# Reordering the last chunks of a convolution stage, moving one tap of two chunks to ScalarE and GpSimd, and issuing two sums earlier

## The chip, the cores and the metric

The kernel runs on one core of a Trainium2 chip. The metric is the device time of one execution in microseconds (us), and the number that counts is the median over the runs. In what follows PE is TensorE (the matrix engine), DVE is VectorE, ACT is ScalarE, POOL is GpSimd, and SP is the engine that only issues DMAs. Each works through its own list of instructions in order and waits for the others by semaphores.

## The reference, cut to what matters

The input `x` is (8, 6400, 128): eight batches, 6400 time steps, 128 channels. First a causal convolution of the full length with a filter `h` (done with FFTs in the reference), then a short convolution of five taps that makes a gate, and a gated projection:

```python
y = np.fft.irfft(np.fft.rfft(x, n=L, axis=1) * np.fft.rfft(h, n=L, axis=0)[None], n=L, axis=1)[:, :S, :]
gate_pre = sum(conv_w[k] * xp[:, k:k + S, :] for k in range(5))   # xp: y with 4 zeros in front
out = ((1 / (1 + np.exp(-gate_pre))) * (y @ w_val)) @ w_out
```

All data is float32.

## The kernel before

**The stages.** A sequence of 6400 is laid out as 100 x 64. For each batch the transform runs in four matmul stages. Stage 1 (`Forward`, lines 240 to 284) takes sums and differences of the two halves of an `x` tile (`sums`, on POOL) and multiplies them (`half`). Stage 2 (`Product`) multiplies by constants, DVE multiplies the result by the spectrum of `h`, and POOL adds the cross terms. Stage 3 (`s3_quads`) goes back. Stage 4 (`Chunk.s4`) gives the convolved sequence in 13 chunks: `HEAD` with 4 of the 64 rows (numbers 60 to 63) and twelve chunks of 5 rows, named by their first row 0, 5, ..., 55. A row is 100 time positions, so a chunk is 128 x 500.

**Two alternating loops per batch.** Lines 643 to 663 run 16 steps. Step g does stage 3 of this batch, stage 1 of the next batch (`fx.half`, `fx.sums`), and pieces of the gate work that the previous batch left over (`steps[g]`). Lines 693 to 736 then run 15 slots s. Slot s does stage 2 of the next batch in 13 blocks (blocks 11 and 12 in slots 7 and 8) and stage 4 of this batch, one chunk a slot, in an order that line 670 makes. In the seven batches that have a successor that order is 60, 0, 35, 40, 45, 50, 55, 5, 10, 15, 20, 25, 30, so that slots 7 to 12 have the chunks 5, 10, 15, 20, 25, 30. The end of this loop, from slot 7 on, is called the tail here; it comes before step 0 of the next loop of 16 steps.

**What a chunk does.** The result of `s4` stands in PSUM. In the same slot `copies` lets ACT copy it to SBUF (`act(self.y, self.p)`) and, unless the chunk is `late` (25 and up), scale it by tap 4 into the gate rows a+4 to a+8 (`init`) and by tap 3 into a spare tile `q` (`keep`). One slot later `taps` lets DVE add taps 0, 1 and 2, read from PSUM, to the gate rows a to a+6. Two slots later `add` lets POOL add `q` to the rows a+3 to a+7. So neighbouring chunks write overlapping gate rows and have to follow each other. A late chunk does only the copy in its slot; its `init`, `keep`, `taps` and `add` run in the steps of the next loop (chunk 25 in steps 0 and 1, 30 in steps 2 and 3, and so on), from the SBUF copy. `HEAD` and chunks 10, 15, 20 (`held`) and the late ones get their projection (`project`), sigmoid (`sigm`), product (`gate`), output matmul (`output`) and store in the steps too (tables `VALUE` and `OUTPUT`). Chunk 5 gets them in slots 10 and 11: in slot 10 PE projects it, ACT takes its sigmoid before the copies of that slot, DVE makes its gate product at the slot's end; in slot 11 PE makes its output.

**What orders the work.** Every instruction keeps the program's order on its engine. PSUM has four buffers of 128 x 500 for `s4`, `project`, `output` and the two results of `half` (`single`), and two double ones for stages 2 and 3 (`pair`). A buffer is taken again when its last reader is done: for a chunk that is not late this is its last DVE tap, for a late one its ACT copy, for a projection its gate product. The SBUF tile `h_sb[3]` holds spectrum block 11 until POOL has used it in slot 7, and its two halves hold the copies that `keep` inside `s3_quads` makes in even and odd steps; `h_sb[0]` holds the `q` tiles of chunks 15 (first half) and 20 (second half), and in steps 0 and 1 ACT issues the DMAs that reload these halves (`ahead`, line 305). `fx.sums` also issues the load of a further `x` tile on SP's queue. The first two sums of the loop of 16 steps (for its steps 0 and 1) are issued at the ends of slots 9 and 10 (line 735), the others inside the steps, always two steps ahead.

Of the kernel before, what the change touches and what calls it, by code (L numbers as in the profile page):

```python
# [17 lines left out]
N1 = 100  # L18
# [12 lines left out]
CH = 5  # L31
HEAD = (60, 4)
CHUNKS = [HEAD] + [(a, CH) for a in range(0, 60, CH)]
NCH = len(CHUNKS)
OUT_ORDER = CHUNKS[1:] + [HEAD]
LATE = 35
HELD = 10
WAIT = 25
BL = 2 * SB * C
M2B = 3  # L40
MH = 6
HB = 4
XB = 3
XH = 8
VALUE = {10: 0, 15: 1, 20: 2, 25: 4, 30: 5, 35: 6, 40: 8, 45: 10, 50: 12, 55: 14}
OUTPUT = {10: 2, 15: 3, 20: 4, 25: 6, 30: 7, 35: 8, 40: 9, 45: 11, 50: 13}
AHEAD = {
    0: (1, 0, 0), 1: (1, 0, 1), 4: (0, 0, 0), 5: (0, 0, 1), 7: (1, 1, 0), 8: (0, 1, 0),
    9: (0, 1, 1), 10: (0, 2, 0), 11: (0, 2, 1), 12: (1, 1, 1), 13: (1, 2, 0), 14: (1, 2, 1),
# [80 lines left out]
def longconv_moe(ctx: ExitStack, tc: tile.TileContext, x, h, r1, m2, r3, m4, w64, out):  # L130
# [26 lines left out]
    h_sb = [ring_at[M2B + i] for i in (2, 0, 1, 3)]  # L157
# [7 lines left out]
    p_t = [cp.tile([128, CH, N1], F32, name=f"p_{i}") for i in range(2)]  # L165
    keeps = p_t + [h_sb[0][:, i : i + CH * N1].rearrange("p (n t) -> p n t", t=N1) for i in (0, BL // 2)]
    rows = [t.rearrange("p a d n -> p (a d n)")[:, : CH * N1].rearrange("p (n t) -> p n t", t=N1) for t in sd_sb]
    hd = dp.tile([NKB, 128, 2 * SB * C], F32, name="hd")

    def weights():  # L170
# [69 lines left out]
    class Forward:  # L240


        def __init__(self, src, dst, xs=x_sb, o=0):
            self.src, self.dst, self.n, self.s, self.i, self.o = src, dst, 0, 0, 0, o
            self.xs = xs[o % len(xs) :] + xs[: o % len(xs)]
# [125 lines left out]
    def s3_quads(d0):  # L371
        pt = pair()
        for q in range(4):
            for c in range(2):
                for r, k in ((0, 0), (1, 0), (1, 1), (0, 1)):
                    d, o = k * HP + d0 + q, (r + k) % 2
                    w = d // 2 * 2 * N1 + c * 2 * HR + d % 2
                    v = pt[o * HP : (o + 1) * HP, k, q * 2 * N2 : (q + 1) * 2 * N2].rearrange("p (b m) -> p b m", b=2)
                    nc.tensor.matmul(
                        v[:, :, c::2],  # L380
                        lhsT=gyf[r * HP : (r + 1) * HP, w : w + 2 * HP - 1 : 2],
                        rhs=r3_sb[r * HP : (r + 1) * HP, c, :],
                        start=True,
                        stop=True,
                    )
        v = pt.rearrange("p k (d b m) -> p b m k d", b=2, m=N2)
        a = d0 // 4 % 2 * 512
        t = h_sb[HB - 1][:, a : a + 512]
        o = dv.rearrange("p n c (k d) -> p (n c) k d", k=2)[:, :, :, d0 : d0 + 4]

        def keep():
            act(
                t.rearrange("p (m c d) -> p m c d", c=2, d=2 * XG)[:, :, ::-1],
                pt.rearrange("p k (d b m c) -> p b m c (k d)", b=2, m=N2 // 2, c=2)[:, 1],
            )

        def join(op, n):
            u = t.rearrange("p (m k d) -> p m k d", k=2, d=XG)
            nc.vector.tensor_tensor(out=n, in0=v[:, 0, 2:], in1=u[:, 2:], op=op)

        def ends():
            act(o[:, 0:2], v[:, 0, :2])
            act(o[:, N2 : N2 + 2], v[:, 1, :2])

        return keep, ends, lambda: join(ADD, o[:, 2:N2]), lambda: join(ALU.subtract, o[:, : N2 + 1 : -1])
# [26 lines left out]
    class Chunk:  # L432


        def __init__(self, b, i, ch, defer):
            self.b, self.i, self.ch = b, i, ch
            a, n = ch
            self.defer = defer
            self.late = defer and WAIT <= a < HEAD[0]
            self.held = defer and HELD <= a < WAIT  # L440
            self.r = None
            self.y = yl[a][:, :n] if a >= LATE else held_y[a] if a >= HELD else dv[:, a : a + n, 0, :N1]

        def s4(self):
# [39 lines left out]
                self.p = self.y  # L484

        def keep(self):
            self.q = p_t[(self.ch[0] - HELD) // CH % 2] if self.late else keeps[(self.i + (self.i // 8 if self.defer else 1)) % 4]
            self.first(3, self.q, self.p)
            if self.r is not None:
                self.first(2, self.r, self.p)  # L490
# [129 lines left out]
    for b in range(B):  # L620
        nxt = b + 1 < B


        steps = collections.defaultdict(list)
        for c in pend:
            a = c.ch[0]
            if a == HEAD[0]:
                t = NS - 1
            else:
                t = VALUE[a]  # L630
            if c.late:
                k = (a - WAIT) // CH
                if not nxt:
                    c.r = rows[k % 3]
                steps[2 * k] += [lambda c=c: c.taps(range(2))]
                steps[2 * k + 1] += [lambda c=c: c.taps(range(2, 4)), c.add]
            steps[t] += [c.project]
            steps[t if a in OUTPUT else NS - 1] += [c.sigm, c.gate]
            if a in OUTPUT:
                steps[OUTPUT[a]] += [c.output]  # L640
                steps[OUTPUT[a] + 1] += [c.store]
        pend = [c for c in pend if c.ch[0] in (HEAD[0], HEAD[0] - CH)]
        for g in range(NS):
            e = s3_quads(4 * g)
            f = []
            if nxt:
                f = fx.half([single(), single()])
                fx.sums(nc.gpsimd)
            for u in e:
                u()  # L650
            if nxt and g in AHEAD:
                ahead(*AHEAD[g])
            for u in f:
                u(act)
            if b == 0:
                next(wgen, None)
                next(wgen, None)
                if g < 8:
                    m4_load(m4_rest[0], g % 2)
                    if g % 2:  # L660
                        m4_rest.pop(0)
            for u in steps[g]:
                u()
        if nxt:
            h_load(HB - 1)
        if b + 2 < B:
            fx = Forward(x[b + 2], gy)


        chs = CHUNKS if not nxt else sorted(CHUNKS, key=lambda c: (c != HEAD, c[0] > 0, c[0] < LATE))  # L670
        cs = [Chunk(b, i, ch, nxt) for i, ch in enumerate(chs)]
        jobs = collections.defaultdict(list)
        for i, c in enumerate(cs):
            if i and not c.late and not c.held:
                jobs[i + 3].append(c)
        if not nxt:
            jobs[NCH + 2].append(cs[0])
        pr = {}

        def s2(kb):  # L680
            if nxt and kb < NKB:
                pr[kb] = Product(kb)
                m2_load(kb + M2B)

        def times(kb):
            if kb in pr:
                pr[kb].mul_u()
                pr[kb].mul_t()
                pr.pop(kb).add()
                h_load(kb + HB)  # L690

        outs, at = [], 0
        for s in range(max(NCH, *jobs) + 2):
            kbs = list(range(at, min(at + 2 - s % 2, NKB))) if nxt else []
            at += len(kbs)
            if s == 0:
                s2(0)
            if s < 2:
                cs[s].s4()
            late = pend[s : s + 1]  # L700
            if late and s == 0:
                late[0].output()
            for kb in kbs[:1]:
                s2(kb + 1)
            if m4_rest:
                m4_load(m4_rest.pop(0))
            for c in jobs[s]:
                c.project()
            if 1 < s < NCH:
                cs[s].s4()  # L710
            for c in outs + late[: s]:
                c.output()
            for c in jobs[s]:
                c.sigm()
            for kb in kbs[:1]:
                times(kb)
            for kb in kbs[1:]:
                s2(kb + 1)
            if s < NCH:
                cs[s].copies()  # L720
            for c in outs + late:
                c.store(p_t[0][:, : c.ch[1]] if s == 0 or nxt and c.ch[0] == CH else None)
            for kb in kbs[1:]:
                times(kb)
            if 0 < s <= NCH and not cs[s - 1].late:
                cs[s - 1].taps()
            if 2 < s < NCH + 2 and not cs[s - 2].late:
                cs[s - 2].add()
            for c in jobs[s]:
                c.gate()  # L730
            outs = jobs[s]
            if b + 2 < B:
                if s == 5:
                    fx.load(XB)
                if s in (9, 10):
                    fx.sums(nc.gpsimd)
        pend = [cs[0]] + [c for c in cs if c.held or c.late]

# [44 lines left out]
```

## Time and profile before

| what | value |
|---|---|
| median of 3 runs | 949.27 us (947.81 to 949.87) |
| profiled execution | 944.9 us |
| its span, first to last instruction | 943.1 us |
| PE busy | 852.3 us, 90% of the span |
| DVE busy | 746.0 us, 79% |
| POOL busy | 579.0 us, 61% |
| ACT busy | 510.3 us, 54% |
| granted TensorE clock, mean | 0.994 |
| one batch, from output matmul of chunk 5 to the next | 106.1 to 109.6 us |

Rows of the timeline are: start, length, engine, line, operation, tiles written and read, shape, count, and in brackets the idle time just before with what ended it. All instructions carry line 117, because a helper issues them; they are told apart by tiles: `pt` is PSUM, `ring` holds most of the gate rows, chunk copies and `h_sb`, `dt` the input of stage 4 and the gate rows under 10, `gy` the data of stages 1 to 3, `sd` the sums, `gl` the gate rows from 35 on. Rows that group instructions give: shape, count | busy us, mean ns of one | idle us before, and what ended it.

### The profile page before, as it was taken

How to read it: one execution, taken by the hardware profiler on the slowest of the kernel's cores; microseconds unless marked ns; L12 is line 12 of the kernel's file. 1: busy time of each engine (PE TensorE's matmuls, PEld its weight loads, DVE VectorE, ACT ScalarE, POOL GpSimd, SP SyncE). 2: the span in 40 equal slices, each digit the busy share in tenths (PEclk: the TensorE clock that was granted, in tenths of full speed). 3: DMA queues.
4: the chain of work that ended last, by engine and by line, in shares of the span. 5: the costliest groups of instructions: out<-in, count | busy, mean ns of one | idle time of the engine just before them, and what ended most of it. 6: DMA issues, size and time to landing. Idle time of an engine off the chain costs nothing. (4 is left out here: it accounts for less than half of the span.)

```text
span 943.1 us, 48025 instructions
## 1 busy us (share of the span) xinstructions
PE 852.3 (90%) x21360; PEld 679.1 (72%) x21360; DVE 746.0 (79%) x1041; ACT 510.3 (54%) x1222; POOL 579.0 (61%) x602
## 2 busy tenths in 40 slices
PE   7799669999999999998999999989999899999897
PEld 6699658865788568965688658865589657885563
DVE  5657658788897988888798878878787787979786
ACT  4532452278624873277624774168723685248776
POOL 5446645866477755775477764876458673864332
PEclk9999899999999999999999999999999999999999
DMA  8786547827494557826584466934586364921112
GB/s 260 255 294 230 191 155 267 298 82 216 152 322 133 167 191 238 277 81 189 164 306 152 148 194 200 312 110 153 165 284 207 114 192 149 324 88 47 66 56 97
DMA packets 79406, 177.42 MB, mean 188 GB/s; under 512 B 14048, under 2 KB 27360, under 8 KB 79200
## 3 DMA queue, kind: packets, MB, share of 16 engines
q1 hardware_dynamic: 67104, 152.33, 47.8%
q10 hardware_dynamic: 12096, 22.03, 7.9%
q8 instruction: 168, 2.75, 1.2%
q14 instruction: 38, 0.31, 0.1%
HBM read 141.56 MB, written 32.77 MB: 185 GB/s over the span
## 5 line engine op out<-in xcount | busy, mean ns | idle before, releaser
L117 POOL TENSOR_TENSOR gy<-gy,ring 128x512 f32<-128x512 f32 (+1 forms) x182 | 220.1, 1239 | 105.8 <-DVE ring L117 50.7
L117 PEld LDWEIGHTS pt<-r_sb,gy 64*64 64x64 f32 x8192 | 141.6, 136 | 107.3 <-issue 69.2
L117 DVE TENSOR_TENSOR dt<-pt,ring 128x496 f32<-128x496 f32 x256 | 159.7, 666 | 65.1 <-ACT dt L117 63.7
L117 PEld LDWEIGHTS pt<-m_sb,dt 128*64 128x64 f32 x4096 | 185.2, 136 | 28.8 <-issue 12.7
L117 PE MATMUL pt<-m_sb,dt 128*64 128x100 f32 x4096 | 193.0, 248 | 7.7 <-DVE ring L117 6.3
L117 PE MATMUL pt<-gy,ring 128*64 128x128 f32 x3008 | 189.1, 278 | 11.7 <-PE pt L117 4.2
L117 POOL TENSOR_TENSOR sd<-x 128x256 f32<-128x256 f32 x236 | 182.1, 801 | 26.2 <-issue 14.8
L117 ACT COPY ring<-pt 128x512 f32<-128x512 f32 (+2 forms) x216 | 129.2, 600 | 122.4 <-PE pt L117 58.0
L117 PEld LDWEIGHTS pt<-gy,ring 128*64 128x64 f32 x3008 | 175.0, 135 | 25.0 <-PE pt L117 13.3
L117 PE MATMUL pt<-r_sb,gy 64*64 64x64 f32 x8192 | 161.1, 225 | 19.9 <-issue 14.6
L117 PE MATMUL pt<-r_sb,sd 50*64 50x100 f32 x4608 | 137.8, 252 | 29.5 <-issue 20.0
L117 DVE TENSOR_TENSOR gy<-pt,ring 128x1024 f32<-128x1024 f32 (+1 forms) x99 | 116.9, 1181 | 54.5 <-PE pt L117 52.5
L117 DVE TENSOR_TENSOR ring<-pt,ring 128x1024 f32<-128x1024 f32 (+2 forms) x131 | 134.5, 1027 | 11.9 <-PE pt L117 2.7
L117 PEld LDWEIGHTS pt<-r_sb,sd 50*64 50x64 f32 x4608 | 114.1, 136 | 36.9 <-issue 26.9
L117 ACT COPY gy<-pt 128x400 f32<-128x400 f32 x248 | 110.6, 500 | 28.2 <-PE pt L117 27.0
L117 ACT COPY yl<-pt 128x500 f32<-128x500 f32 (+1 forms) x89 | 51.1, 574 | 128.8 <-PE pt L117 128.7
L117 POOL TENSOR_TENSOR gl<-gl,p 128x500 f32<-128x500 f32 (+1 forms) x46 | 54.1, 1177 | 103.9 <-DVE gl L117 68.7
L117 ACT COPY dt<-pt 128x16 f32<-128x16 f32 (+2 forms) x310 | 62.7, 255 | 85.8 <-PE pt L117 85.8
L117 DVE SCALAR_TENSOR_TENSOR gl<-yl,w_sb,gl 128x500 f32<-128x500 f32 (+1 forms) x107 | 92.9, 874 | 2.6 <-POOL gl L117 0.4
L117 PE MATMUL pt<-ring,w_sb 128*64 128x500 f32 x320 | 80.7, 599 | 6.9 <-DVE ring L117 6.8
L117 DVE SCALAR_TENSOR_TENSOR ring<-pt,w_sb,ring 128x500 f32<-128x500 f32 (+3 forms) x94 | 63.1, 671 | 5.7 <-ACT ring L117 1.3
L117 POOL TENSOR_TENSOR ring<-ring,p 128x500 f32<-128x500 f32 (+1 forms) x24 | 25.2, 1051 | 47.4 <-DVE ring L117 22.9
(62 smaller groups left out, 794.0 us busy)
## 6 DMA issues: line engine op xcount, KB each, us to landing
ring<-m SPq DMA_DIRECT2D x69, 512.0 KB, 5.9
ring<-hd SPq DMA_DIRECT2D x63, 512.0 KB, 5.0
x<-xl SPq DMA_DIRECT2D x118, 256.0 KB, 3.3
ring<-hd ACTq DMA_DIRECT2D x42, 256.0 KB, 3.1
ring<-m ACTq DMA_DIRECT2D x42, 256.0 KB, 3.7
out<-ring SPq DMA_DIRECT2D x40, 250.0 KB, 3.8
out<-yl SPq DMA_DIRECT2D x40, 250.0 KB, 3.2
hd<-ring SPq DMA_DIRECT2D x8, 512.0 KB, 4.8
```

The lines of the kernel that those rows point to most:

```text
L117: return self._tc.keep_in_program_order(call(*args, **kwargs))
```

## The change

Four things change, all in the seven batches that have a successor:

- The order of the chunks is a written list. Slots 7 to 12 have 5, 10, 25, 15, 20, 30 instead of 5, 10, 15, 20, 25, 30. The same list orders the left-over work inside a step, so that in steps 1 and 4 the pieces of chunk 25 come ahead of those of chunks 15 and 20.
- Chunks 10 and 15 get a second spare tile `r` (the two halves of `h_sb[3]`). ACT scales the chunk by tap 2 into it in `keep`, DVE leaves tap 2 out, and POOL adds `r` to the gate rows in `add`, after `q`.
- The `q` tiles are named by a table, `KEEP`. It gives each chunk the tile that the formula gave it before.
- The first two sums are issued at the ends of slots 7 and 8 instead of 9 and 10, in the six batches in which there is a batch after the next.

```diff
+ORDER = (60, 0, 35, 40, 45, 50, 55, 5, 10, 25, 15, 20, 30)
+KEEP = {0: 1, 5: 3, 10: 1, 15: 2, 20: 3}
...
+    seconds = {
+        a: h_sb[HB - 1][:, i : i + CH * N1].rearrange("p (n t) -> p n t", t=N1) for a, i in ((10, 0), (15, BL // 2))
+    }
...
-            self.r = None
+            self.r = seconds.get(a) if defer else None
...
         def keep(self):
-            self.q = p_t[(self.ch[0] - HELD) // CH % 2] if self.late else keeps[(self.i + (self.i // 8 if self.defer else 1)) % 4]
+            a = self.ch[0]
+            if self.late:
+                self.q = p_t[(a - HELD) // CH % 2]
+            else:
+                self.q = keeps[KEEP[a] if self.defer else (self.i + 1) % 4]
             self.first(3, self.q, self.p)
             if self.r is not None:
                 self.first(2, self.r, self.p)
...
-        chs = CHUNKS if not nxt else sorted(CHUNKS, key=lambda c: (c != HEAD, c[0] > 0, c[0] < LATE))
+        chs = CHUNKS if not nxt else [(a, CH) if a < HEAD[0] else HEAD for a in ORDER]
...
-                if s in (9, 10):
+                if s in (7, 8):
                     fx.sums(nc.gpsimd)
```

## The prediction

> **What bounds the kernel now.** I read the page first, then the totals of the waits of PE.
>
> ```profile
> PE 852.3 (90%) x21360; PEld 679.1 (72%) x21360; DVE 746.0 (79%) x1041; ACT 510.3 (54%) x1222; POOL 579.0 (61%) x602
> ```
> ```profile
> PE pt L117 <- issue: 34.6, 36, 2.7
> PE pt L117 <- DVE ring L117: 15.9, 25, 1.7
> ```
>
> PE is busy for 90% of the span, so the time is PE's work plus its gaps. The largest gap ("issue", 34.6 us) is one in which PE waits for nothing shown; the change adds or takes no PE instruction and cannot be aimed at it. The 15.9 us behind DVE can change. The groups by shape say where these are:
>
> ```profile
> L117 PE MATMUL pt<-ring,w_sb 128*64 128x500 f32 x320 | 80.7, 599 | 6.9 <-DVE ring L117 6.8
> ...
> L117 PE MATMUL pt<-dt,w_sb 128*64 128x500 f32 x96 | 24.9, 590 | 7.1 <-DVE dt L117 6.8 <-DVE ring L117 0.2
> ```
>
> The second row is the output matmul of chunk 5 in the tail, 6.8 us over seven tails. The first is a matmul inside the 16 steps. The timeline of one batch shows both, PE first:
>
> ```profile
> 297.43 1.94 PE L117 MATMUL pt<-m_sb,dt 128*64 128x100 f32 x40 [0.23 <-DVE ring L117]
> 299.85 1.94 PE L117 MATMUL pt<-m_sb,dt 128*64 128x100 f32 x40 [0.48 <-DVE ring L117]
> 302.77 1.06 PE L117 MATMUL pt<-dt,w_sb 128*64 128x500 f32 x4 [0.98 <-DVE dt L117]
> ...
> 309.29 0.87 PE L117 MATMUL pt<-r_sb,sd 50*64 50x100 f32 x32
> ...
> 312.21 0.88 PE L117 MATMUL pt<-r_sb,sd 50*64 50x100 f32 x31
> ...
> 324.52 1.06 PE L117 MATMUL pt<-ring,w_sb 128*64 128x500 f32 x4 [1.37 <-DVE ring L117]
> ```
>
> 297.43 is the fourth chunk of the tail (20), 299.85 the fifth (25), each waiting for a PSUM buffer that DVE still reads; 302.77 is chunk 5's output, waiting for its gate product. In all 0.23 + 0.48 + 0.98 = 1.69 us of idle PE per tail. 309.29 and 312.21 are stage 1 in steps 1 and 2. 324.52 is the projection of chunk 30 in step 5, which waits for the gate product of chunk 25 on DVE: the four buffers are taken in the order in which they came free, and that product frees the next one.
>
> DVE in the same batch:
>
> ```profile
> 302.04 0.67 DVE L117 TENSOR_TENSOR dt<-pt,dt 128x500 f32<-128x500 f32 x1
> 302.63 2.28 DVE L117 SCALAR_TENSOR_TENSOR ring<-pt,w_sb,ring 128x500 f32<-128x500 f32 x3
> 307.50 1.26 DVE L117 TENSOR_TENSOR dt<-pt,ring 128x496 f32<-128x496 f32 x2 [2.60 <-ACT dt L117]
> 308.92 0.68 DVE L117 TENSOR_TENSOR ring<-pt,ring 128x500 f32<-128x500 f32 x1 [0.16 <-POOL sd L117]
> 309.51 2.06 DVE L117 SCALAR_TENSOR_TENSOR ring<-ring,w_sb 128x500 f32<-128x500 f32 x2
> ...
> 323.80 0.67 DVE L117 TENSOR_TENSOR ring<-pt,ring 128x500 f32<-128x500 f32 x1
> ```
>
> 302.04 is chunk 5's gate product, 302.63 the three taps of chunk 20 (0.76 each), 307.50 the first joins of step 0, 308.92 the gate product of chunk 10, 309.51 the first two taps of chunk 25, 323.80 the gate product of chunk 25. Two things matter. DVE has 2.60 us to spare just before step 0. And from 309.51 to 323.80 no row of it shows a wait in brackets: there DVE is the chain, and it ends at the 1.37 us that PE loses in step 5. The group's 6.8 us show that loss in most of the batches, not in this one alone.
>
> **The change part by part.** I follow this batch. POOL and ACT:
>
> ```profile
> 289.46 2.52 POOL L117 TENSOR_TENSOR gy<-gy,ring 128x512 f32<-128x512 f32 x2 [1.33 <-issue]
> 293.37 3.90 POOL L117 TENSOR_TENSOR gy<-gy,ring 128x512 f32<-128x512 f32 x4 [1.39 <-PE pt L117]
> 297.23 0.61 POOL L117 TENSOR_TENSOR dt<-dt,ring 128x200 f32<-128x200 f32 x1
> 299.79 0.83 POOL L117 TENSOR_TENSOR ring<-ring 128x300 f32<-128x300 f32 x1 [1.95 <-DVE ring L117]
> 300.57 1.42 POOL L117 TENSOR_TENSOR sd<-x 128x256 f32<-128x256 f32 x2
> 302.27 1.25 POOL L117 TENSOR_TENSOR ring<-ring,p 128x500 f32<-128x500 f32 x1 [0.28 <-DVE ring L117]
> 303.48 1.42 POOL L117 TENSOR_TENSOR sd<-x 128x256 f32<-128x256 f32 x2
> 305.04 2.46 POOL L117 TENSOR_TENSOR ring<-ring 128x500 f32<-128x500 f32 x2
> 307.46 2.80 POOL L117 TENSOR_TENSOR sd<-x 128x256 f32<-128x256 f32 x4
> ```
> ```profile
> 296.92 1.25 ACT L117 ACTIVATE ring<-pt,w_sb 128x500 f32<-128x500 f32 x2
> 298.05 0.63 ACT L117 ACTIVATE dt<-dt 128x500 f32<-128x500 f32 x1
> 299.41 0.57 ACT L117 COPY ring<-pt 128x500 f32<-128x500 f32 x1 [0.73 <-PE pt L117]
> ...
> 306.74 0.33 ACTq L117 DMA_DIRECT2D ring<-hd  x1
> ...
> 307.42 0.89 ACT L117 COPY gy<-pt 128x400 f32<-128x400 f32 x2
> 308.19 0.64 ACT L117 ACTIVATE ring<-ring 128x500 f32<-128x500 f32 x1
> ```
>
> *Sums sooner.* The row at 293.37 holds the cross terms of blocks 11 and 12. A full block takes 2.52 (289.46), so block 11 ends near 295.9 and block 12's small pair takes the remaining 1.4. The sums of slots 7 and 8 (1.42 each) now stand behind block 11 and behind block 12, so both stand ahead of chunk 5's add in slot 9: 295.9 + 1.42 + 1.4 + 1.42 = 300.1 before its first piece can start, against 297.23. Block 12's cross terms have until step 0 and lose nothing. The two loads that the sums issue go out earlier on SP, past nothing but chunk 5's store; I cost them at nothing, since the only other SP work of the slots after 5 is that store.
>
> *Behind it, ACT.* The sigmoid of chunk 5 (298.05) waits for that first piece: 300.1 + 0.61 = 300.7, so 2.7 us late, ending at 301.4. In slot 10 the copies of the slot's chunk, now 15, are queued behind it on ACT. A copy, then `init`, `keep`, `r` at about 0.57 apart (two take 1.25) put the end of `r` of chunk 15 at 303.6, and chunk 20's `keep` at 305.2.
>
> *Chunk 5's output.* DVE no longer has chunk 15's taps ahead of chunk 5's gate product. That starts at 301.4 instead of 302.04, and PE's output, the chunk after it and step 0 move 0.64 us up. Of the 1.69 us of gaps about 1.05 remain: 0.23 and some 0.8 before the output. This is what the change saves on PE in a tail.
>
> *Two taps off DVE, two adds onto POOL.* DVE saves 2 x 0.76 = 1.5 us, but in a stretch where it now waits. Chunk 10's adds (`q`, `r`, 1.25 each) follow chunk 5's second piece (0.83), which ends near 301.5, and end at 304.0. They touch gate rows 12 to 17, chunk 15's taps rows 15 and up, and slot 10's adds now come ahead of slot 11's taps in the program. So chunk 15's two taps run 304.0 to 305.5 and chunk 20's three to 307.8, where DVE's tail ended at 302.63 + 2.28 = 304.9: 2.9 us later. The joins at 307.50 cover most of that, by their 2.60 of idle time, and start about 0.4 late.
>
> *POOL's adds are late.* Chunk 15's adds share rows with chunk 20's taps and wait for them: `q` ends at 309.1, `r` at 310.3, chunk 20's add at 311.6. Before, the pair at 305.04 ended at 307.50. So they end 4.1 us later, and have no slack. Three things stand behind them. First, the sums for step 2 follow on POOL and end at 313.0; PE wants them at 312.21, so it is 0.8 to 0.9 late there, and the 0.64 of lead is gone. Second, on ACT the DMA of step 0 (306.74) reloads the tile that `q` of chunk 15 is read from; it now waits until 309.1, and the copies at 307.42 and the sigmoid of chunk 10 at 308.19 stand behind it, so they run 1.8 late. One of these copies frees a PSUM buffer for 309.29: 0.4 late. Third, chunk 25's first tap (309.51) writes rows that chunk 20's add writes and starts at 311.6: 2.1 late. As DVE has no wait from there to 323.80, the gate product of chunk 25 is 2.1 late too, and with it the matmul at 324.52 if its buffer is freed by that product again.
>
> *Where the order inside steps changes.* In step 1 chunk 25's last early tap goes ahead of chunk 15's gate product, in step 4 chunk 25's projection ahead of chunk 20's output. The work is the same; what it does is to shift which buffer comes free first. No row shows it, so I bound it by one stage-1 matmul group and its like, 0.9 us either way, and take nothing.
>
> *A rule beside it.* The two taps at 309.51 read only SBUF and took 2.06 where three taps from PSUM took 2.28, that is 2 x 0.76 = 1.52: 0.54 lost beside POOL's sums. The Trainium skill, SBUF — State Buffer, section "SBUF: two separate sides", says that a DVE instruction with two SBUF inputs and a POOL instruction exclude each other for a whole instruction. By that rule a chunk 25 tap that meets one more add of 1.25 would lose that much, and six batches 7.5 us beyond the sum below; by the row the loss is the 0.54 that is already there, because sums run beside these taps in both kernels. The sum goes by the row.
>
> **The sum.** Per batch PE loses between 0.9 us (step 2's sums alone) and 2.1 us (the chain to step 5). I take 1.2, nearer the lower end: where PE is already late by an issue gap, a late buffer costs less, and these gaps are twice the DVE waits in total. Six batches have sums in their tails and a full loop of 16 steps behind them: 6 x 1.2 = 7.2. The seventh has no sums in its tail and no stage 1 after it: chunk 5's sigmoid is on time, and its adds end half a microsecond late or a little early; I take 0. The profiled execution took 944.9 (span 943.1), 4.4 under the median of 949.27, so 952.1 for an execution like it, and 956.5 for the median. I give 956.5. The case's own range is 6 x 0.9 to 6 x 2.1 with half of the lower end open to issue gaps that shrink: 952 to 962.
>
> **The rivals.** All times are medians. About 0.2%, 1.9 us, is what a measurement can tell from no change.
>
> *Faster: the tail's gain stays.* If DVE is what bounds the tail, as the 1.69 us of gaps suggest, two taps fewer take 1.5 off it, PE keeps 0.64 to 1.5 per tail, and seven tails give 4.5 to 10.5: some 943. It decides if chunk 20's add ends by about 309.5 and step 2's sums by 312.2, that is if my chain of POOL is 2 us too long. For it speaks that POOL waits 1.95 us at 299.79 in this batch; against it that the sums fill just this hole, and that everything behind chunk 5's add is in program order. 0.13.
>
> *No change.* The 0.64 gained and the 0.9 lost at step 2 nearly cancel, and step 5 loses nothing because its matmul gets a buffer that is freed sooner. Then 0 to 0.3 per batch: 949 to 951. 0.11.
>
> *Slower by more.* The new order in step 4 makes stage 1 of step 5, 0.9 us ahead of 324.52, wait for chunk 25's gate product as well. Then 2.1 + 0.8 per batch, 17 in all: 967. 0.08.
>
> That the change does not do what it says can be left out: the new table of `q` tiles names the same tiles, and the adds and copies are plainly there.
>
> **How the numbers follow.** Forecast 0.68, faster 0.13, no change 0.11, slower by more 0.08. So faster 0.13, within 0.2% 0.11, slower 0.76. The range takes the forecast whole, reaches over no change down to the nearer part of the faster case, and leaves out 967 and most of what is faster: 946.5 to 962.
>
> **What would show it.** Right: the sigmoid of chunk 5 some 2.7 us later against the product of block 11; the idle 0.98 before chunk 5's output a little smaller; DVE's 2.60 before step 0 gone; chunk 20's add ending after the first joins of step 0; stage 1 of step 2 waiting for POOL's sums; in step 0 the ACT copies of stage 1 waiting with the DMA for POOL. Wrong: step 0 on PE over 1 us earlier and no new PE wait in steps 1 to 5, or chunk 25's first tap no later than now against step 0.

## The result, and the profile after

| | before | after |
|---|---|---|
| median | 948.62 us (947.81 to 949.87, 4 runs) | 958.36 us (957.08 to 963.14, 4 runs) |
| profiled execution, its span | 944.9, 943.1 us | 957.08, 955.3 us |
| granted TensorE clock in it, mean | 0.994 | 0.989 |

The changed kernel is slower: ratio 1.0104, 95% interval 1.0073 to 1.0135, that is 9.7 us by the medians against 7.2 forecast. The page after and its waits of PE:

```profile
PE 859.6 (90%) x21360; PEld 683.3 (72%) x21360; DVE 738.4 (77%) x1027; ACT 515.0 (54%) x1236; POOL 605.3 (63%) x616
```
```profile
PE pt L119 <- issue: 34.2, 33, 3.2
PE pt L119 <- DVE ring L119: 15.0, 24, 1.4
PE pt L119 <- ACT gy L119: 10.0, 13, 1.3
PE pt L119 <- DVE dt L119: 8.6, 11, 2.3
...
PE pt L119 <- POOL sd L119: 2.6, 6, 0.4
```

The helper's line is now 119. The issue gaps are as before (34.6). The row behind DVE's work on `ring` hardly moved (15.9 before), the one on `dt` fell (10.1 before). New are 10.0 us behind ACT's stage-1 copies (2.0 before) and 2.6 behind POOL's sums. PE's busy time is 7.3 us longer with the same instructions; the granted clock of this execution was half a per cent lower, which by that share makes some 4 of these 7.3, an estimate. One profile of each does not show whether the lower clock belongs to the execution or to the change.

The same batch on PE, before and then after, cut at the first stage-3 matmul of step 0 (`pt<-r_sb,gy`) and the first stage-2 matmul of slot 0 (`pt<-gy,ring`):

```profile
411.60 1.19 PE L117 MATMUL pt<-r_sb,gy 64*64 64x64 f32 x64
...
466.65 1.61 PE L117 MATMUL pt<-gy,ring 128*64 128x128 f32 x24 [0.18 <-ACT gy L117]
...
520.75 1.19 PE L117 MATMUL pt<-r_sb,gy 64*64 64x64 f32 x64
```
```profile
416.10 1.06 PE L119 MATMUL pt<-dt,w_sb 128*64 128x500 f32 x4 [0.59 <-DVE dt L119]
...
418.81 1.19 PE L119 MATMUL pt<-r_sb,gy 64*64 64x64 f32 x64
424.30 0.91 PE L119 MATMUL pt<-r_sb,sd 50*64 50x100 f32 x30 [1.34 <-ACT gy L119]
427.75 0.92 PE L119 MATMUL pt<-r_sb,sd 50*64 50x100 f32 x32 [0.43 <-POOL sd L119]
430.69 1.06 PE L119 MATMUL pt<-ring,w_sb 128*64 128x500 f32 x4 [1.04 <-DVE ring L119]
441.30 1.06 PE L119 MATMUL pt<-ring,w_sb 128*64 128x500 f32 x4 [0.16 <-DVE ring L119]
...
476.51 2.07 PE L119 MATMUL pt<-gy,ring 128*64 128x128 f32 x32 [0.17 <-ACT gy L119]
...
529.51 1.19 PE L119 MATMUL pt<-r_sb,gy 64*64 64x64 f32 x64
```

The 15 slots took 520.75 - 466.65 = 54.10 us before and 529.51 - 476.51 = 53.00 after: 1.10 less. The 16 steps took 55.05 before and 476.51 - 418.81 = 57.70 after: 2.65 more. PE's waits for other engines in the steps stand in brackets: 1.34 in step 1, 0.43 and 1.04 in step 2, 0.16 in step 5. The first three are new, and they are the same within 0.02 us in all six loops that follow a changed tail and have stage 1 in them. In step 5 these loops wait 0.16 to 0.84 us; before, five of them waited 0.99 to 1.70 there and the one shown not at all. POOL, ACT and DVE of the changed kernel around step 0 (418.81) show why:

```profile
412.69 1.42 POOL L119 TENSOR_TENSOR sd<-x 128x256 f32<-128x256 f32 x2
414.07 0.61 POOL L119 TENSOR_TENSOR dt<-dt,ring 128x200 f32<-128x200 f32 x1
...
415.42 1.25 POOL L119 TENSOR_TENSOR ring<-ring,p 128x500 f32<-128x500 f32 x1
416.75 1.25 POOL L119 TENSOR_TENSOR ring<-ring 128x500 f32<-128x500 f32 x1
422.10 3.78 POOL L119 TENSOR_TENSOR ring<-ring 128x500 f32<-128x500 f32 x3 [4.10 <-issue]
425.83 3.68 POOL L119 TENSOR_TENSOR sd<-x 128x256 f32<-128x256 f32 x4
```
```profile
417.84 1.28 ACT L119 ACTIVATE ring<-pt,w_sb 128x500 f32<-128x500 f32 x2
...
423.38 0.33 ACTq L119 DMA_DIRECT2D ring<-hd  x1
423.75 0.89 ACT L119 COPY gy<-pt 128x400 f32<-128x400 f32 x2 [2.89 <-POOL ring L119]
424.52 0.64 ACT L119 ACTIVATE ring<-ring 128x500 f32<-128x500 f32 x1
```
```profile
418.04 3.93 DVE L119 SCALAR_TENSOR_TENSOR ring<-pt,w_sb,ring 128x500 f32<-128x500 f32 x5 [1.99 <-POOL ring L119]
421.88 1.25 DVE L119 TENSOR_TENSOR dt<-pt,ring 128x496 f32<-128x496 f32 x2
425.19 0.68 DVE L119 TENSOR_TENSOR ring<-pt,ring 128x500 f32<-128x500 f32 x1 [2.06 <-ACT ring L119]
425.92 2.31 DVE L119 SCALAR_TENSOR_TENSOR ring<-ring,w_sb 128x500 f32<-128x500 f32 x2
...
440.57 0.67 DVE L119 TENSOR_TENSOR ring<-pt,ring 128x500 f32<-128x500 f32 x1
```

418.04 is the start of the five taps of chunks 15 and 20: they wait 1.99 us for POOL, which adds chunk 10's `q` and `r` at 415.42 and 416.75. Only then can POOL add chunks 15 and 20: the profile names no cause for its 4.10 us of idle time, but the adds (422.10) start as the taps end (421.97). ACT stands 2.89 us in front of its DMA at 423.38, the sigmoid of chunk 10 at 424.52 comes late, and DVE's gate product at 425.19 waits 2.06 for it. 425.92 are the first taps of chunk 25, 440.57 is its gate product.

### The profile page after: what moved, and what is told of

The parts are those of the page before. It is cut to its first block, busy times and chain, and to the rows that moved or that the text cites. A ratio compares the mean times of both kernels' runs of the same rounds, so it can differ in the third digit from the quotient of the medians.

```text
span 955.3 us, 48048 instructions
## 1 busy us (share of the span) xinstructions
PE 859.6 (90%) x21360; PEld 683.3 (72%) x21360; DVE 738.4 (77%) x1027; ACT 515.0 (54%) x1236; POOL 605.3 (63%) x616
## 5 line engine op out<-in xcount | busy, mean ns | idle before, releaser
L119 POOL TENSOR_TENSOR sd<-x 128x256 f32<-128x256 f32 x236 | 191.8, 843 | 25.9 <-issue 13.6
L119 PE MATMUL pt<-r_sb,sd 50*64 50x100 f32 x4608 | 144.2, 258 | 34.6 <-issue 17.4
L119 PEld LDWEIGHTS pt<-r_sb,sd 50*64 50x64 f32 x4608 | 118.7, 140 | 43.5 <-issue 21.3
L119 DVE SCALAR_TENSOR_TENSOR ring<-pt,w_sb,ring 128x500 f32<-128x500 f32 (+3 forms) x80 | 52.8, 660 | 20.1 <-POOL ring L119 14.8
L119 POOL TENSOR_TENSOR ring<-ring 128x500 f32<-128x500 f32 (+1 forms) x38 | 43.9, 1162 | 36.7 <-issue 20.5
```

Of the source, the lines that this page charges most:

```text
L119: return self._tc.keep_in_program_order(call(*args, **kwargs))
```

## The experiments

Each ratio is to the kernel before, run beside it on the same chip. Its medians there were 948.62 us beside the change, 952.03 beside the single parts and order and tap, 952.43 beside tap and sums, the moved DMAs, the third sum and the late loads, and 951.14 beside the rest. The rows of one kernel are compared with each other or with their distance from step 0, since issue gaps fall differently in each execution.

**The parts: order, tap, sums.** Three runs take one part each from the whole change, two take two.

```diff
# order alone: ORDER as in the change, and
-            self.r = seconds.get(a) if defer else None
+            self.r = None
-                if s in (7, 8):
+                if s in (9, 10):
# where the order is left out:
-ORDER = (60, 0, 35, 40, 45, 50, 55, 5, 10, 25, 15, 20, 30)
+ORDER = (60, 0, 35, 40, 45, 50, 55, 5, 10, 15, 20, 25, 30)
```

Order alone: 

> Only the new order of the chunks (5, 10, 25, 15, 20, 30); tap 2 stays on DVE, the first sums stay in slots 9 and 10. Theory: with chunk 25 ahead of 15, the copies and taps of 15 and 20 come later, so chunk 20's add on POOL and with it the sums of step 2 and chunk 25's first tap come later; the order alone makes most of the loss, 6 to 10 us slower than before, with a PE wait for ACT in step 1 or for POOL's sums in step 2. Rival POOL (the two added adds are what costs): 0 to 4 us faster than before, no new PE wait in steps 1 and 2. Rival sums (they hold up the sigmoid of chunk 5): the same as for POOL.

Tap alone: 

> Only tap 2 of chunks 10 and 15 by ACT and POOL; old order, sums in slots 9 and 10. Theory: DVE's tail is the chain in the old order, so two taps fewer bring its end forward by up to 1.5 us per tail and the POOL adds take only idle time: 2 to 7 us faster than before. Rival POOL: each added add of 1.25 us stands ahead of the sums for step 2 and of chunk 25's first tap: 5 to 9 us slower. Rival sums: 0 to 4 us faster.

Sums alone: 

> Only the first two sums in slots 7 and 8; old order, tap 2 on DVE. Theory: the sigmoid of chunk 5 comes 2.7 us late on ACT, but in the old order DVE reaches chunk 5's gate product only after chunk 15's taps, so it is hidden: within 2 us of before. Rival sums: ACT's copies behind the late sigmoid make the loss: 5 to 9 us slower. Rival POOL: within 2 us.

Order and tap: 

> The whole change but for the sums, which stay in slots 9 and 10. Theory: as slow as the whole change, 7 to 12 us slower than before; chunk 25's first tap still starts late. Rival sums: no loss, 0 to 4 us faster than before. Rival POOL: 5 to 9 us slower.

Tap and sums: 

> The change without its new order: tap 2 of chunks 10 and 15 by ACT and POOL and the first sums in slots 7 and 8, the chunks in the old order. Theory (the order is what costs; the tap alone gave -8.8 us, the sums alone -4.8): 9 to 14 us faster than before, some 936 to 940. Rival (tap and sums both only fill the same idle time of POOL): as fast as the tap alone, 7 to 9 us faster than before. Rival (the three parts cost together, whatever the order): no faster than before.

| kernel | median us | ratio | 95% interval |
|---|---|---|---|
| order | 961.55 | 1.0099 | 1.0071 to 1.0127 |
| tap | 943.20 | 0.9910 | 0.9873 to 0.9947 |
| sums | 947.22 | 0.9952 | 0.9928 to 0.9977 |
| order and tap | 962.05 | 1.0113 | 1.0083 to 1.0143 |
| tap and sums | 941.35 | 0.9896 | 0.9872 to 0.9921 |
| all three (the change) | 958.36 | 1.0104 | 1.0073 to 1.0135 |

The order carries the whole loss. Without it the other two parts are worth 1.0%, and that kernel beats both the kernel before and the change; with it they are worth nothing. The tap gave 8.8 us, more than the 2 to 7 expected of it. Its interval overlaps that of tap and sums, so a gain of the sums on top of the tap is not shown.

The profiles show where the order costs. With tap and sums alone the 15 slots of the seven batches take 372.3 us in all (379.2 before), and the steps of the six later loops 323.2 (323.3 before): the gain of the tail is kept. The change takes 369.5 and 339.0.

One row of the page shows the difference, the chunk taps read from PSUM, in the kernel before, in the change, and with the tap and the sums alone (after the bar: busy, mean ns of one; then idle before, with what ended most of it):

```profile
L117 DVE SCALAR_TENSOR_TENSOR ring<-pt,w_sb,ring 128x500 f32<-128x500 f32 (+3 forms) x94 | 63.1, 671 | 5.7 <-ACT ring L117 1.3
```
```profile
L119 DVE SCALAR_TENSOR_TENSOR ring<-pt,w_sb,ring 128x500 f32<-128x500 f32 (+3 forms) x80 | 52.8, 660 | 20.1 <-POOL ring L119 14.8
```
```profile
L119 DVE SCALAR_TENSOR_TENSOR ring<-pt,w_sb,ring 128x500 f32<-128x500 f32 (+3 forms) x80 | 52.8, 660 | 12.3 <-ACT ring L119 9.2
```

The last two have the same 80 taps, but with the new order DVE waits 14.8 us for POOL, and with the old order mostly for ACT. The tail of tap and sums alone (DVE, then POOL) shows why:

```profile
412.46 1.51 DVE L119 SCALAR_TENSOR_TENSOR ring<-pt,w_sb,ring 128x500 f32<-128x500 f32 x2 [0.30 <-ACT ring L119]
413.89 0.67 DVE L119 TENSOR_TENSOR dt<-pt,dt 128x500 f32<-128x500 f32 x1
414.62 2.29 DVE L119 SCALAR_TENSOR_TENSOR ring<-pt,w_sb,ring 128x500 f32<-128x500 f32 x3
```
```profile
414.11 1.25 POOL L119 TENSOR_TENSOR ring<-ring,p 128x500 f32<-128x500 f32 x1 [1.00 <-ACT ring L119]
415.44 1.26 POOL L119 TENSOR_TENSOR ring<-ring 128x500 f32<-128x500 f32 x1
417.04 3.80 POOL L119 TENSOR_TENSOR ring<-ring 128x500 f32<-128x500 f32 x3 [0.34 <-issue]
```

A slot issues the taps of the chunk before and then the adds of the chunk before that one. With 10 and 15 in neighbouring slots, chunk 15's taps (412.46) come ahead of chunk 10's adds (414.11) in the program, and POOL waits for DVE: the taps end at 413.97, though the row names ACT, which ended something at about the same time. With chunk 25 between them the adds come first, and DVE waits for POOL. The gate rows overlap, so the program's order decides. The run with the order alone shows the same wait without any second tap:

```profile
420.06 4.71 DVE L119 SCALAR_TENSOR_TENSOR ring<-pt,w_sb,ring 128x500 f32<-128x500 f32 x6 [2.94 <-POOL ring L119]
```

This wait is not the whole of what the order does, because chunk 20 also comes one slot later. Its first tap writes gate row 24 after ACT's `init` of the same chunk has. That `init` is the first of the two instructions at 417.84 in the change (ACT's row above), and of two at 418.43 with the order alone. With some 0.6 us for the `init` and 2.29 for three taps, DVE's tail could not have ended before about 420.8 in the change, where it ended at 421.97, and 421.4 with the order alone, where it ended at 424.77. By this estimate the wait for POOL makes 1.2 of the 3.7 us by which the tail of DVE ends later against step 0 in the change, and 3.4 of 4.9 with the order alone; the later slot makes the rest. Both come with the order. No run turns adds and taps around with the chunks left in their slots, so the two are not separated by an experiment.

**Half of the order.** Chunk 25 goes between 15 and 20 instead, with the tap and the sums.

```diff
-ORDER = (60, 0, 35, 40, 45, 50, 55, 5, 10, 25, 15, 20, 30)
+ORDER = (60, 0, 35, 40, 45, 50, 55, 5, 10, 15, 25, 20, 30)
```

> The tap and the sums of the change, and half of the order: slots 7 to 12 have 5, 10, 15, 25, 20, 30. Chunk 15 has its old slot; chunk 20 is one slot later, as in the whole change. Theory (what counts is when chunk 20's add is done on POOL, because chunk 25's first tap waits for it): chunk 20's copies and taps are as late as in the whole change, its add ends at most 1 us earlier, and ratio to before is 1.003 to 1.010. Rival (what counts is that chunk 15's copies come in the slot behind the late sigmoid of chunk 5, so that its adds and ACT's DMA are late): ratio 0.988 to 0.995, as with the old order.

954.46 us, ratio 1.0025 (0.9993 to 1.0057): no change that can be told from before, but 1.3% over tap and sums alone. It lies just under the theory's 1.003 and far from the rival's 0.995. Chunk 15's adds now stand between its taps and those of chunk 20 (DVE, then POOL):

```profile
418.11 2.29 DVE L119 SCALAR_TENSOR_TENSOR ring<-pt,w_sb,ring 128x500 f32<-128x500 f32 x3 [4.70 <-POOL ring L119]
```
```profile
414.29 3.78 POOL L119 TENSOR_TENSOR ring<-ring 128x500 f32<-128x500 f32 x3
420.83 1.26 POOL L119 TENSOR_TENSOR ring<-ring 128x500 f32<-128x500 f32 x1 [2.75 <-ACT p L119]
```

DVE waits 4.70 us here, more than the 1.99 of the change, and the loss is smaller. What goes with the loss is the end of chunk 20's add on POOL, counted from step 0: 420.84 - 417.32 = 3.5 us with tap and sums alone (0.9896), 422.09 - 416.26 = 5.8 here (1.0025), 425.88 - 418.81 = 7.1 in the change (1.0104). These three kernels all have the tap and the sums; the kernel before, without them, has 2.0 at a ratio of 1, so the end of this add does not set the time by itself.

**Taking away the consequences.** The prediction named three things behind POOL's late adds. The first run here moves ACT's two reload DMAs two steps back, the second also issues the third sum in slot 11.

```diff
-    0: (1, 0, 0), 1: (1, 0, 1), 4:
+    2: (1, 0, 0), 3: (1, 0, 1), 4:
# second run, as well:
-                if s in (7, 8):
+                if s in (7, 8, 11):
```

> The whole change, and the two DMAs that ACT issues in steps 0 and 1 to reload the tiles of chunks 15 and 20 move to steps 2 and 3, so that ACT's copies no longer stand behind POOL's add of chunk 15. Theory of one chain (chunk 25's first tap waits for chunk 20's add, and from there DVE has no slack): PE's wait for ACT in step 1 (1.34 us) goes, and its waits for POOL in step 2 and for DVE after it grow by as much: within 2.5 us of the whole change, 956 to 961. Rival (each of the new PE waits is paid by itself): six times 1.34, 8 us faster than the whole change, some 950.

> As the run before, and a third sum (that of step 2) is issued at the end of slot 11, where POOL is idle for 4 us, so that step 2 does not wait for it; each step's own sum is then that of three steps on. Theory of one chain: the waits for ACT and POOL are both gone and DVE's remain and grow: within 3 us of the whole change. Rival (each wait by itself): 6 x (1.34 + 0.43) = 10.6 us faster than the whole change, some 948, the time of before.

Measured: 964.22 us, ratio 1.0118 (1.0085 to 1.0151), and 964.61 us, 1.0138 (1.0113 to 1.0163). The granted clock was lower in these runs (mean 0.979 and 0.976, before 0.986); the two of the first kernel at 0.982 and 0.987 took 958.77 and 960.25 us. So neither is shown to be worse than the change, and neither is better. By the ratio the first is 1.3 us above the change, within the theory's 2.5, and the second 3.2, just beyond its 3. In microseconds the first lies above the 956 to 961 expected of it, but the kernel before was 3.8 us slower beside it than beside the change. PE of the first, then PE of the second:

```profile
429.12 1.21 PE L119 MATMUL pt<-r_sb,sd 50*64 50x100 f32 x32 [2.14 <-POOL sd L119]
```
```profile
436.09 1.43 PE L119 MATMUL pt<-ring,w_sb 128*64 128x500 f32 x4 [2.91 <-DVE ring L119]
```

The wait for ACT went, and the one for the sums grew from 0.43 to 2.14; that went too, and the one for DVE's gate product grew from 1.04 to 2.91. The three, 1.34 + 0.43 + 1.04 = 2.81 in the change, are one delay seen through three waiters. Step 5 shows where it ends. Its projection of chunk 30 (441.30 in the change) waits for DVE's gate product of chunk 25, and starts 22.5 us after step 0's first stage-3 matmul in all six loops of the change. Before it starts at 19.0 to 21.0, and with tap and sums alone at 18.9 to 19.6. With ACT's DMAs moved it starts at 22.5 to 22.8, and with the third sum as well at 22.1 to 23.7. Whichever wait ahead of it is taken away, PE gets there no sooner on the whole.

The next run takes the third consequence as well: chunk 25's early taps go to steps 1 and 2. A last one also puts the old order inside the steps.

```diff
-                steps[2 * k] += [lambda c=c: c.taps(range(2))]
-                steps[2 * k + 1] += [lambda c=c: c.taps(range(2, 4)), c.add]
+                t0 = 2 * k + (nxt and k == 0)
+                steps[t0] += [lambda c=c: c.taps(range(2))]
+                steps[t0 + 1] += [lambda c=c: c.taps(range(2, 4)), c.add]
```

> The whole change, with all three things that stand behind POOL's late adds taken away at once: ACT's two reload DMAs in steps 2 and 3, the third sum at the end of slot 11, and chunk 25's early taps in steps 1 and 2 instead of 0 and 1, so that DVE does not stand in step 0 until chunk 20's add is done. In the run with only the first two, DVE stood idle from its gate product of chunk 10 (3.6 to 4.2 us after step 0's first stage-3 matmul) to chunk 25's first tap at 7.1, about 2.2 us. Theory (the late adds of POOL act through these three and nothing else): DVE does the joins of step 1 in that idle time, at least 1.5 of the 2.9 us that a batch loses in its steps come back, ratio 1.000 to 1.006, and if the whole of it comes back, with the tail's gain, 0.992 to 0.998. Rival (the loss is not by waits on chunk 20's add but by DVE and POOL working in the same SBUF stretch, or by the order inside the steps): the ratio stays at 1.009 or over.

> As the run with all three consequences taken away, and with the old order inside the steps as well, so that chunk 15's gate product comes ahead of chunk 25's taps. Theory: as that run or up to 0.7 us per batch better, ratio 0.995 to 1.005, since a gate product that frees a PSUM buffer no longer stands behind taps that free none. Rival: within 0.2% of that run, at 1.009 or over.

Measured: 963.49 us, ratio 1.0115 (1.0077 to 1.0154), and 973.26 us, 1.0194 (1.0150 to 1.0237), at a clock of 0.978 and 0.977 in the profiles. The claim that these three are all fails: nothing came back, and step 5's projection of chunk 30 still starts at 22.4 to 22.7. The ratio is the one that the rival gave. Of its two causes the order inside the steps is ruled out below. DVE and POOL slowing each other is not what the order adds either, since with tap and sums alone DVE is busy for 739.3 us and POOL for 604.2, and in the change for 738.4 and 605.3. ACT and DVE of the first run show a fourth consequence:

```profile
430.06 0.59 ACT L119 COPY ring<-pt 128x512 f32<-128x512 f32 x1 [2.37 <-POOL ring L119]
```
```profile
430.83 1.25 DVE L119 TENSOR_TENSOR dt<-pt,ring 128x496 f32<-128x496 f32 x2 [1.78 <-ACT dt L119]
...
438.21 2.21 DVE L119 SCALAR_TENSOR_TENSOR ring<-ring,w_sb 128x500 f32<-128x500 f32 x2 [0.84 <-POOL ring L119]
```

430.06 is the copy for the joins of step 1. It writes the half of `h_sb[3]` in which chunk 15's `r` stands, and waits until POOL has added it; the joins (430.83) follow it 1.78 late. Chunk 30's first tap (438.21) then waits 0.84 for chunk 25's add. So the time that the moved taps left free on DVE could not be used. The second run fits neither of its expectations. With the old order inside the steps chunk 25's first tap starts 8.6 us after step 0 instead of 8.1, and the projection of chunk 30 at 23.3; why that costs this kernel 0.8% and the change nothing is open.

**The order inside the steps,** by itself: the whole change, with chunk 25 behind 15 and 20 inside a step.

```diff
-        pend = [cs[0]] + [c for c in cs if c.held or c.late]
+        pend = [cs[0]] + sorted((c for c in cs if c.held or c.late), key=lambda c: (c.ch[0] < LATE, c.ch[0]))
```

> The whole change, but the left-over work inside a step keeps the order that it had before (chunk 25 behind chunks 15 and 20). The prediction took this order at 0, between -0.9 and +0.9 us per batch. In the profile after, chunk 25's third early tap stands ahead of chunk 15's gate product on DVE in step 1, and PE waits 1.04 us for that product at the projection of chunk 20. Theory (one chain on DVE, which starts late because chunk 20's add on POOL is late): the product of chunk 15 comes 0.7 earlier and the 1.04 falls to some 0.3, but DVE reaches chunk 25's gate product at the same time, and the wait ahead of chunk 30's projection grows by what went; ratio to before 1.007 to 1.012. Rival (the order inside the steps is a large part of the loss): the 1.04 goes and does not come back, at least 0.7 us in each of six batches, ratio 1.003 to 1.006.

961.57 us, ratio 1.0092 (1.0059 to 1.0124), as the theory says.

```profile
431.49 1.06 PE L119 MATMUL pt<-ring,w_sb 128*64 128x500 f32 x4 [0.38 <-DVE ring L119]
...
442.63 1.06 PE L119 MATMUL pt<-ring,w_sb 128*64 128x500 f32 x4 [1.56 <-DVE ring L119]
```

The 1.04 of step 2 falls to 0.38, and the 0.16 of step 5 grows to 1.56. The projection of chunk 30 starts 22.4 us after step 0, where the change has 22.5: the order in the steps chooses where PE waits, and not when it gets past step 5.

**The sums without their loads.** The sums alone gained 0.5%, which no theory had put there. This run has the sums in slots 7 and 8, and leaves the loads behind them in slots 9 and 10.

```diff
+                    fx.sums(nc.gpsimd, False)
+                if s in (9, 10):
+                    fx.load()
```

> The kernel before with the first two sums in slots 7 and 8, but the loads of x that follow them still issued at the ends of slots 9 and 10. The sums alone with their loads gave 4.8 us that I had not expected. If the loads' earlier start is the cause (less DMA traffic beside the steps, fewer issue gaps of PE): the gain goes, within 2 us of before. If POOL's earlier sums are the cause (chunks 15's and 20's adds end 1.4 us earlier): the gain stays, 3 to 6 us faster than before.

944.32 us, ratio 0.9928 (0.9904 to 0.9953), 8.1 us faster and so more than the 3 to 6 expected if the sums are the cause. The earlier start of the loads is not the cause. What is stays open (last section).

## Why the prediction was right, and where its terms were off

It forecast slower, 956.5 us, and 958.36 was measured. Its steps can be checked on the batch above. The second and third column are distances from step 0's first stage-3 matmul (305.48 in the prediction's batch, 418.81 here). The fourth is their difference less the 1.10 us by which step 0 comes sooner, so it is on the scale of the forecast.

| step | before | after | later by | forecast |
|---|---|---|---|---|
| end of chunk 20's taps | -0.57 | 3.16 | 2.63 | 2.9 |
| first join of step 0 | 2.02 | 3.07 | -0.05 | 0.4 |
| ACT's stage-1 copies | 1.94 | 4.94 | 1.90 | 1.8 |
| PE, stage 1 of step 1 | 3.81 | 5.49 | 0.58 | 0.4 |
| POOL, end of chunk 20's add | 2.02 | 7.07 | 3.95 | 4.1 |
| PE, stage 1 of step 2 | 6.73 | 8.94 | 1.11 | 0.8 to 0.9 |
| chunk 25's first tap | 4.03 | 7.11 | 1.98 | 2.1 |
| DVE, gate product of chunk 25 | 18.32 | 21.76 | 2.34 | 2.1 |
| PE, projection of chunk 30 in step 5 | 19.04 | 22.49 | 2.35 | 2.1 |

**The chain** from the adds of chunk 10 to these nine events was right, each within 0.5 us. That it begins with the place of the adds in the program, which the prediction said in passing ("slot 10's adds now come ahead of slot 11's taps"), is in part what the parts show: DVE waits for POOL there with the new order, with or without the second tap, and with the old order the same adds cost less than the taps that they replace. The other part is the later slot of chunk 20. Of the signs that it named as wrong one half came, step 0 over 1 us earlier, and the other, no new wait in steps 1 to 5, did not.

**The sums and chunk 5.** The first piece of chunk 5's add now starts at 414.07, behind both sums, as forecast. In the change that late sigmoid is not what costs: order and tap without the sums is as slow (1.0113).

**Terms that were off.** The lead in a tail is 1.10, not 0.64. Of the gaps 0.23 and 0.59 remain, 0.82 of 1.69 where the forecast had 1.05, so 0.87 went; the other 0.23 us of the lead stands in no gap that was listed. Summed as in the batch above, the steps of the six later loops lose 15.7 us (338.95 against 323.26) and six tails gain 7.7: 8.0 where the forecast had 7.2. Its 1.2 per batch, chosen between 0.9 and 2.1, was 1.3. The reason that it gave, that a late buffer costs less where PE is already late by an issue gap, shows in step 5: the projection of chunk 30 starts at 22.5 in every loop of the change, but before at 19.0 to 19.1 in the two loops that were quickest there, with no issue gap on the way, and at 21.0 in the loop with the most (1.7 us). Less the lead of 1.10 it comes 2.3 us later than in the first and 0.4 later than in the last. How many such gaps an execution has could not be forecast, so that 1.2 came this close is in part luck.

**The seventh batch** was taken at 0, and this step failed. The last loop has no sums and no stage 1, but it has the wait for chunk 10's adds (DVE, then PE):

```profile
855.58 3.93 DVE L119 SCALAR_TENSOR_TENSOR ring<-pt,w_sb,ring 128x500 f32<-128x500 f32 x5 [2.90 <-POOL ring L119]
...
863.48 1.51 DVE L119 SCALAR_TENSOR_TENSOR ring<-ring,w_sb 128x500 f32<-128x500 f32 x2 [2.21 <-POOL ring L119]
```
```profile
866.30 1.20 PE L119 MATMUL pt<-r_sb,gy 64*64 64x64 f32 x64 [2.33 <-DVE dt L119]
```

From its step 0 to the end the kernel takes 98.56 us where it took 95.61, 2.95 more, of which 1.97 had been gained in the tail before: 1.0 net. So the change makes 9.0 us in the two profiles. The remaining 3.2 of their 12.2 lie ahead of step 0 of the first loop (1.55) and in that loop (1.65), where the kernels do not differ: run to run.

**Where PE waits.** The prediction had the delay end in step 5, and it does: the last two rows of the table are its 2.1. But PE meets the same delay in steps 1 and 2 first, 2.81 us in each loop, so that little of it is left as a wait in step 5, where the bracket is smaller than before. A bracket says where PE stood and not what the delay cost. Taking the order inside the steps at 0 was right for this kernel (1.0092 against 1.0104).

**The rule weighed there** (the Trainium skill, SBUF — State Buffer, "SBUF: two separate sides", which limits it to GpSimd instructions that read SBUF, as POOL's adds and sums do): chunk 25's two taps took 2.06 before, 2.31 after, and 1.86 with tap and sums alone, each time beside POOL's sums, and 1.51 in the last batch of the change (the row at 863.48), where POOL stood idle. So a loss beside POOL is there, 0.35 to 0.80 us for the two. The case that the prediction weighed, an added add of 1.25 beside these taps, did not come about: they start only when POOL's adds are done, and no run here shows what it would cost.

**The rivals.** "Faster" (943) said that two taps off DVE let PE keep its gain. With the old order it is what happens: 0.9910 for the tap, 0.9896 with the sums. Its condition, chunk 20's add ending by about 4.0 after step 0 (309.5), is missed in the change (7.07, or 5.97 less the lead), and met with tap and sums alone (3.5). "No change" (949 to 951) wanted step 5 to lose nothing, and "slower by more" (967) wanted stage 1 of step 5 to wait for chunk 25's gate product. Step 5's projection comes 2.35 later by the table, and the last piece of its stage 1 (440.54 in the loop above) starts before that product does (440.57).

## What to carry to other kernels

When chunks that add into overlapping rows are reordered, write down for each pair of neighbours which engine's update now stands first in the program: putting a chunk between them can turn "POOL waits for DVE" into "DVE waits for POOL" without an instruction more. A delay that shows as waits for several engines may be one delay; follow it to the last place where it is waited for, compare when that place is reached, and take away one waiter to see whether the next one grows, before mending any. Parts of a change do not add up: here two of three gained 1.0% together, and the third cost 2% on top of them, so each part is worth a run of its own.

## What the runs showed that was not expected

Issuing the two sums two slots sooner, with nothing else changed, makes the kernel 0.5% faster (0.7% with the loads left behind), while PE's waits for DVE did not fall:

```profile
PE pt L119 <- issue: 28.9, 29, 3.5
PE pt L119 <- DVE ring L119: 17.4, 28, 1.5
PE pt L119 <- DVE dt L119: 10.0, 11, 1.3
```

The issue gaps are 28.9 us where before had 34.6, and the slots take the same time (378.9 and 379.2 in all), so the gain lies in the steps (318.8 and 323.3 in the six later loops). But the change with the old order inside the steps has 29.3 too, and is slower, so one profile each does not show that they carry the gain. The cause is open.
